# Three edits and a reordering in the front half of a fused attention and feed-forward kernel: V of one tile pair by seven products, separate PSUM tiles for the halves of a transpose, a narrower wait for one weight load, and VectorE's side work in another order

## The chip, the cores and the metric

The kernel runs on one core of a Trainium2 chip. The metric is the device time of one execution in microseconds (us); lower is better. TensorE (PE) multiplies matrices, VectorE (DVE) and ScalarE (ACT) work on rows of 128 partitions, GpSimd (POOL) and SyncE (SP) help, and DMAs are issued from SP's and ACT's queues. Matmuls write to PSUM, a small memory that VectorE and ScalarE must empty.

## The reference, cut to what matters

```python
def _A_ref(x, wqkv, wo):                      # linear attention, 32 heads of 32
    q, k, v = split(x @ wqkv)
    phi = lambda t: jnp.where(t > 0, t + 1, jnp.exp(t)) + 1e-6
    pq, pk = phi(q), phi(k)
    kv = einsum("bhsd,bhse->bhde", pk, v);  z = sum over s of pk
    o = (pq @ kv) / (pq . z + 1e-6)
    return o @ wo
def _B_ref(x, w_gate, w_up, w_down):
    return (silu(x @ w_gate) * (x @ w_up)) @ w_down
xn = layernorm(x)
out = x + _A_ref(xn, ...) * silu(_B_ref(xn, ...))
```

x is 2048 rows of 1024 in bf16; the feed-forward part is 3584 wide.

## The kernel before

There are three stages. The first normalises x, transposes it to xnT (the 1024 features on the partitions, two SBUF tiles of 1024 rows each), and computes K, V, the sums kv and z, and most of Q. The second computes the attention output o, writes it to DRAM, reads it back transposed (oT) and multiplies it by wo. The third is the feed-forward part, the longest; the change does not touch it.

The 2048 rows are 16 tiles of 128, in 4 blocks of 512. In the first stage a step on tile i is one of these:

- `emit_stats`, `emit_rstd`, `emit_N`: mean, variance and normalising, on VectorE.
- `emit_T(i)`: tiles 0 to 7 are transposed on TensorE, eight 128x128 transposes into the PSUM tile `tr_ps`; VectorE copies the first four of them to xnT (L423), ScalarE the other four (L424). Blocks 2 and 3 (tiles 8 to 15) go another way: `emit_xT_block` stores the normalised block to DRAM and a DMA transposes it back (L427, L428), both on SP's queue.
- `emit_B(i, c)`: one quarter of K and V for a tile, eight matmuls of 512 columns (L444) into a PSUM tile `kv_ps`. For K (c of 0, 1) ScalarE takes exp and relu (L186, L187) and VectorE makes phi of them (L190, L191); for V (c of 2, 3) ScalarE casts to `v_sb` (L462).
- `emit_C(i)`: eight matmuls of 129 columns (L473) that add phi(K)-transposed times V, and z, to the PSUM tiles `kvz`.

Tiles 0 to 8 and tile 12 are done so. For Q, and for the tile pairs (10,14) and (11,15) of K and V and (9,13) of K, the kernel saves an eighth of the matmuls: a 2x2 block product by seven products of half the depth instead of eight. `QGroup(p, m)` and `KVGroup(which, t)` are such groups; which = 0 is K, 1 is V, written K(t), V(t) and Q(p, m) here; Q(0, 2) is part 2 of the first half of the rows. Each product is four matmuls of 512 columns (L131), 28 for a group instead of 32. `part_a` makes M3 into X and M4 into Y, `part_b` M1 into Z and adds M5 to X and M2 to Y, `part_c` adds N7 to X and N6 to Y. Between them ScalarE copies X to `qu`, VectorE adds Y and Z to it (L236 and L241 for Q, L544 and L549 for K and V), ScalarE takes the two results that are done after M5 and M2, and VectorE subtracts for the other two after N7 and N6 (L251 for Q, L561 for K, L564 for V). A product that adds to X or Y has to wait until the readers before it are done.

The operands of these products are sums that VectorE makes ahead of time: five sums of x for each half of the rows (`xsum_ops`, L138), four of each of four wq parts (`wsum_ops`, L152 to L155), five of wk and five of wv (`kv_sum_ops`, L499 to L503). Places for them are found in SBUF that is no longer read; three of wv's lie in quarters of xnT. V of tiles 9 and 13 is computed by `VPlain`, which calls `emit_B` four times.

The order of the first two stages is written out by hand (`tc.manual_schedule`), and every engine keeps it. VectorE's side work (statistics and norms of blocks 2 and 3, then the sums) stands in a queue `later`; `put(weight, ops)` adds to it, and `fill(n)` gives credit and takes operations off while credit is left:

```python
        def fill(n):
            credit[0] += n
            while later and credit[0] > 0:
                weight, op = later.popleft()
                credit[0] -= weight
                op()
```

In the loop over `rest` (tiles 4 to 8 and 12), `fill` is called four times a tile with the numbers of `nf`; in the list `seq` each group has two numbers, `fa` after `part_a` and `fb` after `part_b`. In `seq` a group's `part_a` comes before the `part_c` of the group ahead of it, and `emit_C` of a pair follows when both its K and its V are ready (`have`).

PSUM in these two stages: pool `psA` has three buffers, `psB` five, each of one 2 KiB bank; kv_ps, tr_ps, the X, Y and Z of the groups and s_ps take turns in psB.

In the second stage the pools of the first are closed and new ones opened over the same SBUF: `wop` (for `wo_sb`), `p2oT` (for oT), `p2work`, `p2small`. By default a tile of a new pool waits for all that used the closed pools' space; with `reuse_waits="tile"` it waits for the users of its own place alone. `wo_sb` lies where `wk_sb` lay. SP's queue carries the two loads of `wo_sb` (L868) and then the transposing reads of oT (L831), whose data ACT's queue stores (L830). `emit_ND` makes o of a tile (`nd_ps`, `o_sb`), `emit_S` the product with wo (`s_ps`, L844).

Of the kernel before, what the change touches and what calls it, by code (L numbers as in the profile page):

```python
# [13 lines left out]
FP16 = mybir.dt.float16  # L14
# [7 lines left out]
def kernel(  # L22
# [12 lines left out]
    P = 128  # L35
# [175 lines left out]
    class QGroup:  # L211
# [17 lines left out]
        def part_a(self):  # L229
            self.X = psB.tile([P, CW], FP32, name="qX", tag="B")  # L230
            self.mm(self.X, "M3", True)
            self.u = qtmp.tile([P, CW], FP32, name="qu", tag="qu")
            nc.scalar.copy(out=self.u[:], in_=self.X[:])
            self.Y = psB.tile([P, CW], FP32, name="qY", tag="B")
            self.mm(self.Y, "M4", True)
            nc.vector.tensor_tensor(out=self.u[:], in0=self.u[:], in1=self.Y[:], op=ALU.add)  # L236
# [10 lines left out]
        def part_c(self):  # L247
            for acc, which, i in ((self.X, "N7", 0), (self.Y, "N6", 1)):
                self.mm(acc, which, False)
                e, r = self.er(i, i)  # L250
                nc.vector.tensor_tensor(out=r, in0=self.u[:], in1=acc[:], op=ALU.subtract)  # L251
                emit_exp_relu(e, r, r)
# [11 lines left out]
    with ExitStack() as p1:  # L264
# [136 lines left out]
        def emit_T(i):  # L401

            h = DC // 2
            dst = xn_tok_ap(i)
            xn = xn_slot(i)

            def tr(t_ps, dcs):
                for k, dc in enumerate(dcs):
                    nc.tensor.transpose(t_ps[:, k, :], xn[:, dc * P:(dc + 1) * P], ident[:])

            if i == 0:
                tr_a = psB.tile([P, h, P], FP16, name="tr_ps", tag="B")[:]
                tr_b = psB.tile([P, h, P], FP16, name="tr_ps", tag="B")[:]
                emit_norm(i, xn[:, 0:h * P], cols=slice(0, h * P))
                tr(tr_a, range(0, h))
                emit_norm(i, xn[:, h * P:D], cols=slice(h * P, D))
                tr(tr_b, range(h, DC))
                nc.scalar.copy(out=dst[:, 0:h, :], in_=tr_a)
                nc.scalar.copy(out=dst[:, h:DC, :], in_=tr_b)
            else:  # L420
                tr_ps = psB.tile([P, DC, P], FP16, name="tr_ps", tag="B")
                tr(tr_ps, range(DC))
                nc.vector.tensor_copy(out=dst[:, 0:h, :], in_=tr_ps[:, 0:h, :])  # L423
                nc.scalar.copy(out=dst[:, h:DC, :], in_=tr_ps[:, h:DC, :])  # L424

        def emit_xT_block(b):
            nc.sync.dma_start(out=blk_rows_pt(xn_dram, b), in_=xn_blk_slot(b))  # L427
# [37 lines left out]
        def emit_B(i, c):  # L465
            emit_B_mm(i, c)
            emit_B_out(i, c)
# [119 lines left out]
        def put(weight, ops):  # L587
            later.extend((weight, op) for op in ops)
# [19 lines left out]
        def put_sums():  # L608

            alloc_pqT()  # L610
            k_ops = kv_sum_ops(0, (pq_place(NPASS - 1, NM_Q - 2), pq_place(NPASS - 1, NM_Q - 1), x_quarter(0, 0, 1)))
            v_ops = kv_sum_ops(1, (x_quarter(0, 1, 0), x_quarter(1, 0, 1), x_quarter(1, 1, 0)))
            put(2, xsum_ops(0))
            put_ws(0)
            put_ws(1)
            put(2, xsum_ops(NPASS - 1))
            put(2, k_ops)
            put_ws(2)
            put(2, v_ops[:1])
            put_ws(3)  # L620
            put(2, v_ops[1:])

        put_stats(NB - 2)
        put(1, [lambda: emit_rstd((NB - 2) * TPB)])
# [6 lines left out]
        with tc.manual_schedule(engines=FRONT_ORDER | {ET.SP}):  # L631

            warm_up(14)
            emit_stats(0, parts=(0,))
            emit_stats(0, parts=(1,))
            emit_aggr(0)
            emit_rstd_act(0)
            emit_T(0)
            emit_stats(1)
            warm_up(2)  # L640
            emit_B_mm(0, 0)
            emit_rstd_act(1)
            nc.scalar.preload_act_table(ACT.Exp)
            emit_N(1)
            emit_T(1)
            ln(2)
            emit_B_mm(1, 0)
            emit_B_out(0, 0)
            emit_B_mm(0, 1)
            emit_B_out(1, 0)  # L650
            emit_B_mm(1, 1)
            ln(3)
            emit_N(2)
            emit_B_out(0, 1)
            emit_B_mm(0, 2)
            emit_T(2)
            emit_B_out(1, 1)
            emit_B_mm(1, 2)
            emit_B_out(0, 2)
            emit_N(3)  # L660
            emit_B_mm(2, 0)
            emit_B_out(1, 2)
            emit_B_mm(2, 1)
            emit_stats(TPB)
            emit_T(3)
            emit_stats(TPB + 1)
            emit_rstd(TPB)
            emit_B_out(2, 0)
            emit_B_mm(2, 2)
            emit_B_out(2, 1)  # L670
            emit_stats(TPB + 2)
            emit_B_mm(0, 3)
            emit_B_out(2, 2)
            emit_B_mm(1, 3)
            emit_B_out(0, 3)
            emit_stats(TPB + 3)
            emit_rstd(TPB + 2)
            emit_C(0)
            emit_B_mm(2, 3)
            emit_B_out(1, 3)  # L680
            emit_N(TPB)
            emit_N(TPB + 1)
            emit_C(1)
            emit_B_mm(3, 0)
            emit_B_out(2, 3)
            emit_C(2)
            emit_B_out(3, 0)
            emit_B_mm(3, 1)
            fill(4)
            emit_T(TPB)  # L690
            emit_B_out(3, 1)
            emit_N(TPB + 2)
            emit_N(TPB + 3)
            emit_B_mm(3, 2)
            emit_T(TPB + 1)
            emit_B_out(3, 2)
            fill(2)
            emit_B(3, 3)
            fill(2)

            rest = list(range(TPB, 2 * TPB)) + [b * TPB for b in range(2, NB)]
            fills = {rest[-1]: (2, 3, 2, 2)}
            before = TPB - 1
            for i in rest:
                nf = fills.get(i, (3, 2, 2, 2))
                grp = QGroup(0, 0) if i == rest[-1] else None
                emit_B(i, 0)
                fill(nf[0])
                emit_C(before)
                before = i  # L710
                if grp:
                    grp.part_a()
                emit_B(i, 1)
                fill(nf[1])
                if grp:
                    grp.part_b()
                if i == TPB:
                    emit_T(TPB + 2)
                emit_B(i, 2)
                fill(nf[2])  # L720
                if i == TPB:
                    emit_T(TPB + 3)
                if grp:
                    grp.part_c()
                emit_B(i, 3)
                if grp:
                    grp.post()
                fill(nf[3])

            K, V = (lambda t: KVGroup(0, t)), (lambda t: KVGroup(1, t))  # L730
            class VPlain:


                def part_a(self):
                    emit_B(tiles1[0], NCC)

                def part_b(self):
                    for i, c in ((tiles1[0], NCC + 1), (tiles1[1], NCC), (tiles1[1], NCC + 1)):
                        emit_B(i, c)

                def part_c(self):
                    have(tiles1)

                def post(self):
                    pass

            tiles1 = [(NB - 2 + j) * TPB + 1 for j in range(2)]
            Q = QGroup
            seq = [(lambda: Q(0, 1), 1, 1), (VPlain, 4, 6), (lambda: K(1), 1, 1), (lambda: Q(0, 2), 1, 1),
                   (lambda: V(2), 3, 3), (lambda: K(2), 1, 1), (lambda: Q(0, 3), 1, 0), (lambda: K(3), 0, 0),  # L750
                   (lambda: Q(NPASS - 1, 0), 0, 0), (lambda: V(3), 0, 0), (lambda: Q(NPASS - 1, 1), 0, 0)]
            prev = None
            for make, fa, fb in seq:
                grp = make()
                grp.part_a()
                fill(fa)
                if prev:
                    prev.part_c()
                    prev.post()
                else:  # L760
                    emit_C(before)
                if make is not seq[-1][0]:
                    grp.part_b()
                    fill(fb)
                while ready_C:
                    emit_C(ready_C.popleft(), last=(not ready_C and make is seq[-1][0]))
                prev = grp
            qa = prev
            assert not later
# [1 line left out]
        gate(wq_loads, marks[("B", 3)], sync=True)  # L771

    with ExitStack() as p2:
        wop = p2.enter_context(tc.tile_pool(name="wop", bufs=1))
        otp = p2.enter_context(tc.tile_pool(name="p2oT", bufs=1))
        work = p2.enter_context(tc.tile_pool(name="p2work", bufs=2))
        small = p2.enter_context(tc.tile_pool(name="p2small", bufs=2))
# [499 lines left out]
```

## Time and profile before

| | us |
|---|---|
| median of three runs | 756.86 (754.5 to 758.6) |
| the profiled execution | 754.58 |
| its span, first to last instruction | 752.8 |
| TensorE busy in the span | 744.0 |
| VectorE, ScalarE busy | 508.3, 276.1 |
| tile 4's C (the pause at kvz) | starts 49.48 |
| first product of Q, last C | 80.07, 158.15 |
| first product with wo | 171.79 |
| feed-forward part begins | 239.97 |

The granted clock of TensorE is 1.000 throughout. Times in the profile are counted from the first instruction. A matmul's record reaches beyond the start of the next, since they are pipelined (0.379 us each for 512 columns); what a stretch costs is seen from starts. A line "idle before <- X" or "waited for" names what ended the wait.

### The profile page before, as it was taken

The numbers are of one execution on the slowest core, as the hardware profiler recorded it, in microseconds if no ns is written. First come the engines' busy times: TensorE is split into PE (matmuls) and PEld (weight loads), VectorE is DVE, ScalarE is ACT, GpSimd is POOL, SyncE is SP. The second block draws the span as 40 slices with busy tenths as digits, with TensorE's granted clock in tenths as the row PEclk, the third lists the DMA queues.
The fourth block names the chain that finished last, engine by engine and source line by source line (L and its number), as shares of the span: only waits on it lengthen the run. The fifth ranks groups of instructions, "written<-read, shape, count | busy, mean of one in ns | idle before, by whom it ended". The sixth has DMA issues, their size and how long they took to land.

```text
span 752.8 us, 9958 instructions
## 1 busy us (share of the span) xinstructions
PE 744.0 (99%) x3744; PEld 350.2 (47%) x3744; DVE 508.3 (68%) x939; ACT 276.1 (37%) x483; POOL 51.1 (7%) x101
## 2 busy tenths in 40 slices
PE   9999999999999999999999999999999999999997
PEld 4544444454554444444444444444444444444454
DVE  6788887687754667886777767876755844445453
ACT  4444555754324434333343434343343111111111
POOL 3310000000000000000000000000000222122220
PEclk9999999999999999999999999999999999999999
DMA  9617000045589633764345733544869845554200
GB/s 313 221 39 211 1 1 0 1 137 144 173 226 293 175 104 106 203 182 124 107 147 163 220 100 105 175 148 129 286 227 347 304 181 182 181 182 167 99 29 29
DMA packets 127664, 115.99 MB, mean 154 GB/s; under 512 B 29440, under 2 KB 108416, under 8 KB 126336
## 3 DMA queue, kind: packets, MB, share of 16 engines
q1 hardware_dynamic: 122720, 106.58, 45.5%
q10 hardware_dynamic: 4896, 8.78, 3.3%
q8 instruction: 29, 0.48, 0.3%
q14 instruction: 19, 0.16, 0.1%
HBM read 70.52 MB, written 38.54 MB: 145 GB/s over the span
## 4 chain that ended last, share of the span: by engine, by line
PE 94%; DVE 3%; DMA 1%; ACT 1%; issue 0%; DVEq 0%; ACTq 0%
PE X L131 29%; PE Y L131 29%; PE Z L131 10%; PE kv_ps L444 9%; PE s_ps L844 7%; PE qY L131 2%; PE qX L131 2%; PE kX L131 2%; PE kY L131 1%; PE nd_ps L807 1%; PE kvz L473 1%; DVE stats L335 1%; PE w_ps L482 1%; DMA o_dram<-o_sb 1%; PE kZ L131 1%; PE qZ L131 1%
## 5 line engine op out<-in xcount | busy, mean ns | idle before, releaser
L131 PEld LDWEIGHTS <-ws_all 128*128 128x128 bf16 x1420 | 137.6, 98 | 161.8 <-issue 0.2
L940 DVE TENSOR_TENSOR q<-n,Y 128x512 f32<-128x512 f32 x63 | 43.4, 688 | 107.4 <-PE Y L131 103.9
L131 PEld LDWEIGHTS <-xs 128*128 128x128 bf16 (+1 forms) x716 | 67.6, 98 | 74.4
L1210 POOL TENSOR_TENSOR o_out<-y,xres 128x512 bf16<-128x512 f32 x29 | 35.2, 1215 | 665.9 <-DVE y L1209 665.9
L131 PE MATMUL Y<-xs,ws_all 128*128 128x512 f16 (+3 forms) x308 | 70.3, 360 | 0.0
L131 PE MATMUL X<-xnT,ws_all 128*128 128x512 f16 (+1 forms) x280 | 70.2, 379 | 0.0
L131 PE MATMUL X<-xs,ws_all 128*128 128x512 f16 x224 | 57.5, 379 | 0.0
L131 PE MATMUL Z<-xs,ws_all 128*128 128x512 f16 x224 | 57.5, 379 | 0.0
L131 PE MATMUL Y<-xnT,ws_all 128*128 128x512 f16 x224 | 57.5, 379 | 0.0
L1064 ACT ACTIVATE g<-cg 128x512 bf16<-128x512 f32 x56 | 35.3, 631 | 53.6 <-DVE cg L955 53.6
L946 DVE TENSOR_TENSOR u<-Z,q 128x512 f32<-128x512 f32 x63 | 43.2, 686 | 16.0 <-PE Z L131 15.9
L1064 ACT ACTIVATE g<-X 128x512 bf16<-128x512 f32 x28 | 16.7, 597 | 99.7 <-PE X L131 99.7
L444 PEld LDWEIGHTS <-xnT 128*128 128x128 f16 x352 | 33.7, 98 | 39.0 <-DVE xnT L423 0.7
L936 ACT COPY n<-X 128x512 f32<-128x512 f32 x63 | 36.9, 586 | 28.7 <-PE X L131 28.7
L444 PE MATMUL kv_ps<-wv_sb,xnT 128*128 128x512 bf16 x192 | 44.0, 379 | 0.0
L1089 DVE TENSOR_TENSOR ho<-g,up 128x1024 bf16<-128x1024 bf16 x56 | 38.2, 685 | 0.5
L444 PE MATMUL kv_ps<-wk_sb,xnT 128*128 128x512 bf16 x160 | 37.3, 379 | 0.5 <-DVE xnT L423 0.5
L1209 DVE TENSOR_TENSOR y<-y,s_in 128x512 f32<-128x512 f32 x31 | 22.2, 717 | 20.6 <-ACT y L1203 15.8
L131 PEld LDWEIGHTS <-wg_sb 128*128 128x128 bf16 x224 | 21.9, 98 | 26.4
L131 PEld LDWEIGHTS <-wu_sb 128*128 128x128 bf16 x224 | 21.9, 98 | 26.4
L848 ACT CAST s_sb<-s_ps 128x512 bf16<-128x512 f32 x32 | 18.5, 586 | 39.4 <-PE s_ps L844 33.0
L844 PE MATMUL s_ps<-wo_sb,oT 128*128 128x512 bf16 x128 | 29.4, 379 | 1.6 <-DMA oT<-o_dram 1.6
(179 smaller groups left out, 1109.0 us busy)
## 6 DMA issues: line engine op xcount, KB each, us to landing
h_dram<-ho SPq DMA_DIRECT2D x56, 256.0 KB, 2.5
wg_sb<-in_B_w_gate_dram SPq DMA_DIRECT2D x14, 512.0 KB, 4.0
wu_sb<-in_B_w_up_dram SPq DMA_DIRECT2D x14, 512.0 KB, 4.6
wdr<-in_B_w_down_dram SPq DMA_DIRECT2D x14, 512.0 KB, 4.2
ws_all<-h_dram SPq DMA_DIRECT2D x4, 1792.0 KB, 8.9
wds_dram<-wdsA SPq DMA_DIRECT2D x14, 384.0 KB, 2.8
hp_a<-h_dram SPq DMA_DIRECT2D x3, 1792.0 KB, 8.3
o_dram<-o_sb ACTq DMA_DIRECT2D x16, 256.0 KB, 3.0
```

What stands on the lines that cost most here:

```text
L131: marks["mm"] = nc.tensor.matmul(acc[:, 0:c1 - c0], lhsT=lhs(k), rhs=rhs(k)[:, c0:c1], start=(first and k == 0), stop=(k == n - 1), skip_g ...
L335: nc.vector.bn_stats(out=part_stats[i][:, c, :], in_=xr[:, c, :])
L444: mm = nc.tensor.matmul(kv_ps[:], lhsT=xn_tok_ap(i)[:, dc, :], rhs=wkv_ap(c)[:, dc, :], start=(dc == 0), stop=(dc == DC - 1))
L844: mm = nc.tensor.matmul(s_ps[:], lhsT=oT[:, c, ttok], rhs=wo_sb[:, c, cc * CW:(cc + 1) * CW], start=(c == 0), stop=(c == G - 1))
L848: nc.scalar.copy(out=s_sb[:, cc * CW:(cc + 1) * CW], in_=s_ps[:])
L936: nc.scalar.copy(out=n[:], in_=self.X[:])
L940: nc.vector.tensor_tensor(out=self.q[:], in0=n[:], in1=self.Y[:], op=ALU.add)
L946: nc.vector.tensor_tensor(out=self.u[:], in0=Z[:], in1=self.q[:], op=ALU.add)
L1064: nc.scalar.activation(out=self.g[:, i, j * TB:(j + 1) * TB], in_=src, func=ACT.Silu)
L1089: nc.vector.tensor_tensor(out=self.ho[:, i], in0=self.g[:, i], in1=self.up[:, i], op=ALU.mult)
L1209: nc.vector.tensor_tensor(out=t[:], in0=t[:], in1=self.s_in[:, i, cs], op=ALU.mult)
L1210: (nc.vector if last and (i, j) != (0, 0) else nc.gpsimd).tensor_tensor(out=self.o_out[:, i, cs], in0=t[:], in1=self.xres[:, i, cs], op=AL ...
```

## The change

- `emit_T` puts the two halves of a transpose in two PSUM tiles, each a buffer of psB, for all tiles but tile 0, where it was so already.
- `VPlain` is gone; V of tiles 9 and 13 is V(1), after Q(0, 2) in `seq`, and K(2), V(2), Q(0, 3) follow in a slightly different order. The order of `put_sums` has all five sums of wv ahead of the last wq part.
- `fills`, the default of `nf` and the numbers in `seq` give more credit in tiles 5 to 12 and less in `seq`.
- `wop` is opened with `reuse_waits="tile"`.

Line numbers of the changed kernel are higher by 2 behind `emit_T`, and lower by 16 in the second stage. On TensorE the order then has 3740 matmuls instead of 3744.

```diff
--- before.py
+++ after.py
@@ -418,10 +418,12 @@
                 nc.scalar.copy(out=dst[:, 0:h, :], in_=tr_a)
                 nc.scalar.copy(out=dst[:, h:DC, :], in_=tr_b)
             else:
-                tr_ps = psB.tile([P, DC, P], FP16, name="tr_ps", tag="B")
-                tr(tr_ps, range(DC))
-                nc.vector.tensor_copy(out=dst[:, 0:h, :], in_=tr_ps[:, 0:h, :])
-                nc.scalar.copy(out=dst[:, h:DC, :], in_=tr_ps[:, h:DC, :])
+                tr_a = psB.tile([P, h, P], FP16, name="tr_ps", tag="B")
+                tr_b = psB.tile([P, h, P], FP16, name="tr_ps", tag="B")
+                tr(tr_a, range(0, h))
+                tr(tr_b, range(h, DC))
+                nc.vector.tensor_copy(out=dst[:, 0:h, :], in_=tr_a[:])
+                nc.scalar.copy(out=dst[:, h:DC, :], in_=tr_b[:])
 
         def emit_xT_block(b):
             nc.sync.dma_start(out=blk_rows_pt(xn_dram, b), in_=xn_blk_slot(b))
@@ -616,9 +618,8 @@
             put(2, xsum_ops(NPASS - 1))
             put(2, k_ops)
             put_ws(2)
-            put(2, v_ops[:1])
+            put(2, v_ops)
             put_ws(3)
-            put(2, v_ops[1:])
 
         put_stats(NB - 2)
         put(1, [lambda: emit_rstd((NB - 2) * TPB)])
@@ -699,10 +700,10 @@
             fill(2)
 
             rest = list(range(TPB, 2 * TPB)) + [b * TPB for b in range(2, NB)]
-            fills = {rest[-1]: (2, 3, 2, 2)}
+            fills = {TPB: (3, 2, 2, 3), 2 * TPB: (5, 3, 2, 2), rest[-1]: (3, 4, 2, 2)}
             before = TPB - 1
             for i in rest:
-                nf = fills.get(i, (3, 2, 2, 2))
+                nf = fills.get(i, (3, 3, 2, 2))
                 grp = QGroup(0, 0) if i == rest[-1] else None
                 emit_B(i, 0)
                 fill(nf[0])
@@ -728,26 +729,9 @@
                 fill(nf[3])
 
             K, V = (lambda t: KVGroup(0, t)), (lambda t: KVGroup(1, t))
-            class VPlain:
-
-
-                def part_a(self):
-                    emit_B(tiles1[0], NCC)
-
-                def part_b(self):
-                    for i, c in ((tiles1[0], NCC + 1), (tiles1[1], NCC), (tiles1[1], NCC + 1)):
-                        emit_B(i, c)
-
-                def part_c(self):
-                    have(tiles1)
-
-                def post(self):
-                    pass
-
-            tiles1 = [(NB - 2 + j) * TPB + 1 for j in range(2)]
             Q = QGroup
-            seq = [(lambda: Q(0, 1), 1, 1), (VPlain, 4, 6), (lambda: K(1), 1, 1), (lambda: Q(0, 2), 1, 1),
-                   (lambda: V(2), 3, 3), (lambda: K(2), 1, 1), (lambda: Q(0, 3), 1, 0), (lambda: K(3), 0, 0),
+            seq = [(lambda: Q(0, 1), 1, 0), (lambda: K(1), 1, 0), (lambda: Q(0, 2), 1, 1), (lambda: V(1), 2, 2),
+                   (lambda: K(2), 0, 0), (lambda: V(2), 2, 1), (lambda: Q(0, 3), 0, 0), (lambda: K(3), 0, 0),
                    (lambda: Q(NPASS - 1, 0), 0, 0), (lambda: V(3), 0, 0), (lambda: Q(NPASS - 1, 1), 0, 0)]
             prev = None
             for make, fa, fb in seq:
@@ -771,7 +755,7 @@
         gate(wq_loads, marks[("B", 3)], sync=True)
 
     with ExitStack() as p2:
-        wop = p2.enter_context(tc.tile_pool(name="wop", bufs=1))
+        wop = p2.enter_context(tc.tile_pool(name="wop", bufs=1, reuse_waits="tile"))
         otp = p2.enter_context(tc.tile_pool(name="p2oT", bufs=1))
         work = p2.enter_context(tc.tile_pool(name="p2work", bufs=2))
         small = p2.enter_context(tc.tile_pool(name="p2small", bufs=2))
```

## The prediction

> **What bounds the kernel now.** I read the page first, for the busy shares and the chain that ended last:
>
> ```profile
> PE 744.0 (99%) x3744; PEld 350.2 (47%) x3744; DVE 508.3 (68%) x939; ACT 276.1 (37%) x483; POOL 51.1 (7%) x101
> PE 94%; DVE 3%; DMA 1%; ACT 1%; issue 0%; DVEq 0%; ACTq 0%
> ```
>
> TensorE is idle for 8.8 us of the span, 1.2 of them before the first matmul and about 4.9 behind the last. Only fewer matmuls, or a shorter pause between two of them, can shorten the run. The view of who waited for whom names the pauses, with SyncE's long wait from the DMA queue's own:
>
> ```profile
> ACT xnT L424 <- DVE xnT L423: 14.6, 7, 3.3
> PE s_ps L844 <- DMA oT<-o_dram: 1.6, 1, 1.6
> PE kv_ps L444 <- DVE xnT L423: 0.5, 1, 0.5
> PE kvz L473 <- ACT v_sb L462: 0.5, 1, 0.5
> SPq L868 <- PE kvz L473: 86.4, 1, 86.4
> ```
>
> TensorE's timeline shows each at its place (start, us, what, idle before):
>
> ```profile
> 9.25 0.61 PE L409 MATMUL tr_ps<-ident,ws_all 128*128 128x128 f16 x8
> 10.38 5.35 PE L444 MATMUL kv_ps<-wk_sb,xnT 128*128 128x512 bf16 x24 [0.52 <-DVE xnT L423]
> ...
> 49.48 0.39 PE L473 MATMUL kvz<-v_sb,pk_sb 128*128 128x129 bf16 x4
> 50.37 0.39 PE L473 MATMUL kvz<-v_sb,pk_sb 128*128 128x129 bf16 x4 [0.50 <-ACT v_sb L462]
> 50.60 1.89 PE L444 MATMUL kv_ps<-wk_sb,xnT 128*128 128x512 bf16 x8
> ...
> 115.06 1.36 PE L473 MATMUL kvz<-v_sb,pk_sb 128*128 128x129 bf16 x16
> 116.26 1.02 PE L131 MATMUL kX<-wv_sb,xs 128*128 128x512 bf16 x4
> ...
> 169.21 1.02 PE L131 MATMUL qY<-xs,ws_all 128*128 128x512 f16 x4
> 171.79 1.90 PE L844 MATMUL s_ps<-wo_sb,oT 128*128 128x512 bf16 x8 [1.55 <-DMA oT<-o_dram]
> ```
>
> Four 512-column matmuls start 0.864 us apart (kX to kY), 0.216 each; a kvz matmul or a transpose takes 0.058 (eight in 0.46). The loss is counted in starts, not in the idle column. The kvz at 49.48 take 1.12 instead of 0.46: 0.66 lost. The sixteen at 115.06 take 1.20 instead of 0.93: 0.27, and the same again at 134.39 (1.20). From 169.21 to 171.79 stand 2.58 instead of 0.86: 1.72. The chain of waits tells why the last is so long:
>
> ```profile
> 163.45 4.98 DMA o_dram<-o_sb
> 168.44 3.30 DMA oT<-o_dram
> 171.79 1.90 PE s_ps L844 x8
> ```
>
> **Part by part.** *Seven products for tiles 9 and 13.* Four plain blocks of 8 matmuls become 28: four fewer, 4 x 0.216 = 0.86 us off the path, for certain. VectorE gets four operations of 0.69 more (2.4 us at their spacing of 0.61), ScalarE one evacuation less; beside 6.0 us of matmuls they hide, if the queues are not already late (below). All five sums of wv existed for tiles 10, 11, 14, 15; they only come earlier.
>
> *Two PSUM tiles per transpose.* ScalarE's half no longer waits for VectorE's. At 47.52 ScalarE had stood 2.83 us for it with tile 4's v_sb behind, which makes the pause at 50.37: 0.66 back. For tile 1 VectorE's half starts four transposes sooner (4 x 0.058): 0.23 back. A transpose now takes two of psB's five buffers. The tightest reuse is the block that starts at 46.03: it needs the buffer of the transpose at 43.41, whose copy follows ScalarE's pair at 43.61 and 44.10 and ends near 45.2. It costs nothing, with 0.6 us to spare; without that cover, one copy of 0.59.
>
> *wo by tile.* The load lies where wk_sb lay. It waited for all of the earlier pools, that is for the last kvz (issue at 158.70), and then ran beside the first store of o_sb, which took 4.98; the view of DMA issues gives such stores 2.1 at best and a median of 2.4 up to 180. Waiting for its own place alone, it leaves after K(3)'s last product with wk_sb, which starts at 144.22: 13 us sooner, into a stretch with a DMA share of 0.01. SyncE has nothing behind it until the transpose at 168.44, which inherits the pool's waits; those end with that kvz too, ten us before its data. The store then lands at 163.45 + 2.4, oT 3.3 later: 169.2, where TensorE is ready at 170.07. All 1.72 go; with a store as slow as before, none. What is late next is oT of the second tile: transpose issued near 170.5, landed by 173.8, wanted at 178.04 - 1.72. [...]
>
> *The accumulations of two tiles.* C of tiles 9 and 13 stood right behind K(1)'s phi and lost 0.27; now V(1) stands between, and at 134.39 likewise V(2) before Q(0,3). Between V(1)'s last product and C stand K(2)'s 12 matmuls, 2.6 us, while its two subtractions need 1.5, so 0.54 are back; if they came late, nothing.
>
> Gains: 0.86 + 0.66 + 0.23 + 1.72 + 0.54 = 4.0.
>
> *Side work sooner.* The order of the instructions shows what moves in front of what; VectorE and ScalarE wait in their places. Two spots have no spare:
>
> ```profile
> 92.59 0.57 ACT L462 CAST v_sb<-kv_ps 128x512 bf16<-128x512 f32 x1
> 93.02 0.62 PE L473 MATMUL kvz<-v_sb,pk_sb 128*128 128x129 bf16 x8
> 123.09 0.57 ACT L535 CAST v_sb<-kX 128x512 bf16<-128x512 f32 x1
> 124.03 1.03 PE L131 MATMUL kX<-wv_sb,xs 128*128 128x512 bf16 x4
> ```
>
> (a) C of tile 12: its fifth matmul needs the cast that ends at 93.16, and starts at 93.25. Between tile 12's phi and the subtraction L251 that ScalarE follows, VectorE had three sums of 1.14 (their spacing, five in 5.76); now two sums and four parts of a w sum (0.34 + 0.60 + 0.34 + 0.34): 3.90 against 3.42. So 0.48 later, 0.09 of it spare: 0.4 lost.
> (b) V(1)'s N7 must wait until ScalarE has read kX. Chain from the end of K(1)'s M4: to VectorE's qu 0.27, qu 0.61, a sum of wv that now stands there 1.14, L251 0.69; ScalarE's four steps from SBUF 2.38, four from PSUM 1.92, copy 0.62; VectorE from L236 to L241 4.45 (111.02 to 115.65 less a wait of 0.18), then 0.60, a sum 1.14, qu 0.61, a sum 1.14, L251 0.71; ScalarE's four 2.38, cast 0.57; handshakes 0.11. Together 19.3. TensorE has 84 matmuls in between, 18.1: 1.2 lost. Before, the plain V blocks stood ahead of this stretch, and sixteen kvz (1.20) inside it.
>
> Bounds of both together: 0, as in the rows above, where both arrive in time, and 2.7, if one more sum (1.14) stands ahead of ScalarE. I take 1.6, the sum of the chains, since each link is a row. [...]
>
> Sum: -4.0 + 1.6 = -2.4. The profiled execution, 754.58 (span 752.8 and 1.8 around it), becomes 752.2. It lies 2.3 under the median of the three runs, 756.86; on that median the forecast is **754.5**.
>
> **Rivals.** *No new waits:* -4.0, 752.9. For it: VectorE idles 1.79 at 75.26 and 1.18 at 53.16, room to get ahead. Against: it is 82% busy from 80 to 120.
> *The store stays slow:* -2.4 + 1.72 = -0.7, 756.2. For it: nothing but that the first store is also the first of its kind; against: the DMA share.
> *VectorE becomes the bound from tile 8 to V(2):* the sums of the second x half (L138) now stand four in a row ahead of tile 8's phi. The second needs the transposed block 3, which landed at 68.18 + 6.1 = 74.3. If it does not land sooner, phi ends at 74.3 + 3 x 1.14 + 1.2 = 78.9, against C of tile 8 at 79.61 - 0.89 = 78.7, and all that is later comes one for one onto TensorE. If then each of wv's five sums (5.7) and the four parts of a w sum (1.6) stand ahead of what ScalarE waits for, 7.3 are lost: +3.3, 760.2. It decides from 4.0 us of new waits. Against: block 2's norms now stand ahead of a phi, so its store and all behind it leave up to 2.3 us sooner.
> *The change does not do what it says:* the wait of wo could still hold it, or tiles 9 and 13 save nothing; the order shows four matmuls fewer and the wait on wk_sb's last reader, so 756 at most.
>
> **How the numbers follow.** Forecast 0.42, no new waits 0.32, slow store 0.10, VectorE 0.12, not as said 0.04. A measurement of this kernel can tell about 0.5% from no change, 3.8 us; the three runs alone lie 4.1 apart. The forecast is 1.4 short of that bound, so some 0.3 of it would be read as faster, and 0.6 of the second case: 0.13 + 0.19, rounded to 0.33. Slower takes a little over half of VectorE's case: 0.07. The rest, 0.60, is the same. The range goes from the second case less two us of scatter, 750.8, to the slow store with 1.4 above, 757.6; it leaves out VectorE's case and the ends of the scatter.
>
> **What would show it.** Right: 3740 matmuls; wo's issue near 144; no pause before the first s_ps; no wait of xnT L426 for VectorE; kvz at tile 4 in 0.46; new pauses at tile 12's C and at V(1)'s N7. Wrong: pauses of over 4 us in all between 75 and 120, a first store near 5 us, or TensorE waiting for a psB buffer between 35 and 50.

## The result and the profile after

The changed kernel takes 752.41 us, the median of six runs (752.04 to 752.71). The kernel before, run beside it, takes 757.73 (six runs, 754.5 to 758.6). The ratio is 0.9938, 95% interval 0.9921 to 0.9956: 0.6% shorter. The forecast was 754.5 with a range of 750.8 to 757.6; the profiled execution, forecast at 752.2, took 752.22 (span 750.4 against 752.8).

So there are two results. The step from the one profiled execution to the other is 2.4 us, as worked out. The step between the medians is 5.3, and 2.9 of it were not foreseen. The busy times on the page of the changed kernel:

```profile
PE 741.2 (99%) x3700; PEld 350.0 (47%) x3740; DVE 510.0 (68%) x943; ACT 274.9 (37%) x482; POOL 51.6 (7%) x101
```

The weight loads (PEld) show the 3740 matmuls; 40 matmul records are missing from this trace. The view of waits, TensorE's and ScalarE's (what waited, for what, us in total, times, longest):

```profile
PE kX L131 <- ACT v_sb L537: 0.6, 1, 0.6
PE kv_ps L446 <- DVE xnT L425: 0.3, 1, 0.3
PE kvz L475 <- ACT v_sb L464: 0.3, 1, 0.3
...
ACT xnT L426 <- PE tr_ps L409: 8.5, 5, 3.1
```

The wait of s_ps for oT is gone, and so is every wait of ScalarE's half of a transpose for VectorE's. What is left at kvz is another tile's wait than before, and the one at kX is new. TensorE's timeline gives the places, and SyncE's the load and the first transpose:

```profile
49.30 0.63 PE L475 MATMUL kvz<-v_sb,pk_sb 128*128 128x129 bf16 x8
...
92.18 0.39 PE L475 MATMUL kvz<-v_sb,pk_sb 128*128 128x129 bf16 x4
92.84 0.39 PE L475 MATMUL kvz<-v_sb,pk_sb 128*128 128x129 bf16 x4 [0.27 <-ACT v_sb L464]
...
116.76 1.02 PE L131 MATMUL kX<-wv_sb,xs 128*128 128x512 bf16 x4 [0.57 <-ACT v_sb L537]
...
168.62 1.02 PE L131 MATMUL qY<-xs,ws_all 128*128 128x512 f16 x4
169.48 1.89 PE L828 MATMUL s_ps<-wo_sb,oT 128*128 128x512 bf16 x7
```

```profile
144.69 1.01 SPq L852 DMA_DIRECT2D wo_sb<-in_A_wo_dram  x2
165.44 1.24 SPq L815 DMA_TRANSPOSE oT<-o_dram  x1
```

Tile 4's C runs through, and C of tiles 9 and 13 takes 0.93 (it starts at 121.07, the next product at 122.00). Tile 12's C loses 0.43 (from 92.18 to qZ at 93.07 are 0.89 instead of 0.46). The product N7 of V(1) starts 1.60 behind kY, which starts at 115.16, instead of 0.86: 0.74 lost, the largest of five delays in that stretch. And s_ps follows qY after 0.86, where it was 2.58: wo's load leaves at 144.69, the first store at 163.14, and the transpose 2.30 behind that, where it was 4.98. In windows of 2 us from 160 to 166 the DMA share, 0.99, 1.07 and 1.05 in the kernel before, is 0.00, 0.02 and 0.34; from 146 to 152 it is 0.88, 1.03 and 1.09.

### The profile page after: what moved, and what is told of

Its sections match the earlier page's. It is cut to its first block, busy times and chain, and to the rows that moved or that the text cites. A ratio compares the mean times of both kernels' runs of the same rounds, so it can differ in the third digit from the quotient of the medians.

```text
span 750.4 us, 9920 instructions
## 1 busy us (share of the span) xinstructions
PE 741.2 (99%) x3700; PEld 350.0 (47%) x3740; DVE 510.0 (68%) x943; ACT 274.9 (37%) x482; POOL 51.6 (7%) x101
## 4 chain that ended last, share of the span: by engine, by line
PE 95%; DVE 2%; ACT 1%; issue 1%; DVEq 0%
PE X L131 29%; PE Y L131 29%; PE Z L131 10%; PE kv_ps L446 8%; PE s_ps L828 7%; PE qY L131 2%; PE qX L131 2%; PE kY L131 2%; PE kX L131 2%; PE nd_ps L791 1%; PE kvz L475 1%; PE w_ps L484 1%; PE qZ L131 1%; PE kZ L131 1%; PE tr_ps L409 0%
## 5 line engine op out<-in xcount | busy, mean ns | idle before, releaser
L131 PEld LDWEIGHTS <-xs 128*128 128x128 bf16 (+1 forms) x736 | 69.6, 98 | 77.8 <-issue 1.4
L446 PEld LDWEIGHTS <-xnT 128*128 128x128 f16 x320 | 30.5, 98 | 35.0 <-ACT xnT L418 0.5
L446 PE MATMUL kv_ps<-wv_sb,xnT 128*128 128x512 bf16 x155 | 36.4, 379 | 0.2
L1187 ACT ACTIVATE y<-X 128x512 f32<-128x512 f32 x8 | 4.8, 597 | 69.7 <-PE X L131 61.2
```

What stands on the lines that cost most here:

```text
L131: marks["mm"] = nc.tensor.matmul(acc[:, 0:c1 - c0], lhsT=lhs(k), rhs=rhs(k)[:, c0:c1], start=(first and k == 0), stop=(k == n - 1), skip_g ...
L446: mm = nc.tensor.matmul(kv_ps[:], lhsT=xn_tok_ap(i)[:, dc, :], rhs=wkv_ap(c)[:, dc, :], start=(dc == 0), stop=(dc == DC - 1))
```

## The experiments

What had to be explained is the 2.9 us that the profiles don't show, and the scatter: the runs of before lay 4.1 apart, those of the changed kernel 0.7. **Theory A**: the pause ahead of the first s_ps is of another length in every execution, and the profiled one was a short one. **Theory B**: the terms of the profile hold in every run, and the rest comes from another part of the change.

The first four kernels shared a chip. There the kernel before took 755.07 (32 runs, 753.91 to 758.38).

**wo by tile alone**, on the kernel before:

```diff
-        wop = p2.enter_context(tc.tile_pool(name="wop", bufs=1))
+        wop = p2.enter_context(tc.tile_pool(name="wop", bufs=1, reuse_waits="tile"))
```

> The kernel before with one edit, wo's pool waiting by tile. The profiled executions of before and after differ by 2.4 us, the timed medians by 5.3 (757.7 against 752.4), and the runs of before lie 4.1 apart, those of after 0.7. Theory A (the store): what varies in before is the first o_sb store, which shares the DMA engines with wo's load; its profiled execution, 754.58, was a lucky one. Then this edit alone removes the scatter and more than 1.72 us: 5.3 less the 0.7 that the rest of the change is worth in the profile gives 4.6, about 753.1, with runs within 1 us. Theory B (the terms of the profile hold in every run, and what else the medians differ by belongs to another part of the change or to how the runs were taken): 1.7 off, about 756.0, and the scatter of some 4 us stays. Both: the load leaves near 144, the store lands in about 2.1 to 2.4, no pause before the first s_ps.

753.12 (752.68 to 753.58), ratio 0.9966 [0.9952, 0.9981]. The scatter is gone with this edit alone, as theory A says. The gain is 1.95 on this chip, close to theory B's 1.7; the 4.6 of theory A were counted from the first set, where before stood higher. In the profiled execution the four stores up to 176 land a median of 2.7 behind their issue, later than the 2.1 to 2.4 expected, and s_ps still follows qY after 0.86.

**All but wo**: the changed kernel with that one line taken back.

> The changed kernel with wo's pool waiting for all the earlier pools again, all else as changed. Theory A: 4.6 slower than after, about 757.0, and the runs 3 to 4 us apart as those of before; the pause before the first s_ps is back and is as long as the store is late. Theory B: 1.7 slower than after, about 754.1, and runs within 1 us of one another.

756.21 (753.92 to 756.54), ratio 0.9998 [0.9983, 1.0013]: without wo's edit nothing is left of the gain. In the profiled executions the last qY starts 0.51 sooner than in the kernel before (168.70 against 169.21), but the first s_ps 0.21 later (172.00 against 171.79): what the first stage gains goes into the pause. Theory A again, but the runs showed more than it had said. They do not spread; they stand in two groups, four at 753.9 to 754.1 and seven at 756.2 to 756.5, with one at 755.6. The mean granted clock of the upper group is 0.996 to 0.997, that of the others 0.998 to 1.000. This mean tells a drop in one direction only: the profiled execution with the transposes alone (below) has 0.998, and its eight s_ps behind the pause take 1.90, as without a drop. It also counts time without work: in the trace of the changed kernel the clock is 0.91 from 748.0 to the end of the span at 750.4, where no matmul runs. By an estimate from the windows below (1.66 us of clock missing in a span of 754.6), one drop like that is worth 0.002. So, by the same estimate, 0.996 and 0.997 show a drop, and 0.998 neither shows nor excludes one. The profiled execution, 756.37, is of the upper group. Its chain of waits, and the view of windows (start and end, length, busy time of PE, PEld, DVE, ACT, POOL with the number of instructions, then TensorE's granted clock, DMA share, GB/s):

```profile
163.21 5.07 DMA o_dram<-o_sb
...
168.29 3.65 DMA oT<-o_dram
...
172.00 3.52 PE s_ps L828 x8
```

```profile
172.00:174.00 2.00, 2.00 (x5) 0.72 (x6) 0.00 (x0) 0.90 (x2) 0.00 (x0) 0.50 0.56 177
174.00:176.00 2.00, 2.00 (x13) 1.02 (x12) 0.26 (x2) 0.44 (x1) 0.00 (x0) 0.67 0.12 29
```

TensorE was idle for 2.27 us here, and behind that its clock was 0.50 from 172 to 174, 0.67 in the next window and 1.00 from 176 on: the first eight s_ps took 3.52 instead of 1.89. The pause is paid once as waiting, 2.44 from start to start, and once more as 1.63 of slow matmuls; together 4.07, where this execution and that of the changed kernel lie 4.15 apart (756.37 and 752.22).

**The transposes alone**: the kernel before with the first hunk of the change.

> The kernel before with the transposed tiles in two PSUM tiles alone. Its two terms are 0.66 at tile 4's accumulation (kvz start to start 0.46 instead of 1.12) and 0.23 at tile 1's first product. Theory A: 0.9 off, about 756.8, scatter as in before. Theory B with the transposes as what steadies the runs: 0.9 and up to 2.9 more, about 753.9, with runs within 1 us.

753.96 (753.08 to 756.38), ratio 0.9984 [0.997, 0.9999]. That is 1.1 under the kernel before on this chip (by the interval 0.1 to 2.3), with its scatter: the size of the term, 0.9, agrees, and theory B's steadying is not there. One of its runs took 756.38 at a mean clock of 1.000: part of the scatter has no drop in it. The absolute figures expected belonged to the first set, where before stood higher.

**The kernel before again.**

> The kernel before, unchanged, for its scatter and for a second profiled execution. Theory A: again 754 to 759; the profiled execution of whatever length has its first store at 4.98 plus what its span has over 752.8, and the pause before the first s_ps at 1.55 plus the same. Theory B: where its span is longer, the additional time stands at other places (x's first loads, or PE's clock), and the first store takes 5 as before.

754.85 (753.97 to 758.09). The profiled execution, 753.97, has the shorter pause that theory A asks for, 0.45 under the 1.55 of the first profile, with a span 0.6 shorter and a store of 4.56 instead of 4.98:

```profile
171.20 1.90 PE L844 MATMUL s_ps<-wo_sb,oT 128*128 128x512 bf16 x8 [1.10 <-DMA oT<-o_dram]
```

This gave two new theories. **C**: a pause costs twice once it is long enough, as the 2.27 was and the 1.10 and 1.55 were not, through the clock. **D**: the clock is only a sign of a long pause, whose length explains all. Two experiments put work in the pause, and one made pauses of known length. Filler in the kernel before (on a chip where that took 754.91, 17 runs, 753.9 to 757.61):

```diff
+            f_ps = psB.tile([P, CW], FP32, name="f_ps", tag="B")
+            for _ in range(8):
+                nc.tensor.matmul(f_ps[:], lhsT=warm[:, 0:P], rhs=warm[:], start=True, stop=True)
             rows = deque((grp, i) for grp in (qa, qb, qc) for i in range(2))
```

> The kernel before with eight more 512-column matmuls that nobody reads, between the last qY product and the first s_ps, where TensorE waits for oT: 1.73 us of work in the pause. In the trace of the changed kernel without wo's edit the idle of 2.27 there was followed by a granted clock of 0.50 to 0.67 for some three microseconds, and eight s_ps matmuls took 3.52 instead of 1.89; after idles of 1.10, 1.16 and 1.55 in other traces the clock stayed at 1.00. Theory C (the pause costs twice: itself, and a clock that halves once it is longer than about two): with the filler the idle that is left is at most 2.2 even in the longest runs, the clock stays at 1.00, the runs of before that lay at 756.3 to 758.4 come down by 1.6, and the short ones go up by up to 0.6 (1.73 of filler against an idle of 1.1 to 1.5): all of them from 754.2 to 756.8, median about 755. Theory D (the scatter is the store's length alone, the clock only a sign of it): short runs up by up to 0.6, the long ones stay at 756.3 to 758.4.

755.66 (754.33 to 756.83), ratio 1.0006 [0.9993, 1.0018], no run with a clock under 0.998. The range is the one of theory C, but only 3 of the 17 runs of before lay above 756.83, too few to decide. The median is 0.7 above that of before: where the pause is short, the filler only delays. And runs of 756.83, 756.44 and 756.23 had a clock of 0.999 or 1.000, with no room for a drop by that estimate, so some 2.5 us of scatter come without the clock. Wo by tile alone took the scatter away, so it should be the pause's length, which was not measured run by run.

**Pauses of known length**, in the feed-forward part of the changed kernel, ahead of M3 of every second group:

```diff
+        nc.tensor.matmul(acc[:, 0:P], lhsT=warm[:, 0:P], rhs=pz[:, 0:P], start=True, stop=True)
+        ...  # GpSimd adds to pz over 128 to 1536 columns
+        nc.tensor.matmul(acc[:, 0:P], lhsT=warm[:, 0:P], rhs=pz[:, 0:P], start=True, stop=True)
```

> The changed kernel with 32 pauses of TensorE in the feed-forward, one ahead of every second group (some 12 us apart), each as long as GpSimd takes for additions over 128, 256, 384, 512, 640, 768, 1024 and 1536 columns, in turn, four times; a short matmul on either side holds the pause. From the row of o_out (512 columns in 1.21) they are some 0.5 to 4 us long, 55 to 60 us in all. Theory C: behind pauses of up to 1.55 the granted clock stays at 1.00 and the next four matmuls start 0.86 apart; behind the longest it drops to 0.50 and costs about 1.6 more each; in between lies the limit, between 1.55 and 2.27, sharp or not. With the 768, 1024 and 1536 columns over the limit, twelve drops of 1.6, 19 us on top of the pauses. Theory D: no drop follows a pause as such; the time is that of the pauses alone.

846.58, one run; 68.5 us of it are the idle time of the 32 pauses. TensorE's timeline behind two pauses of the same 2.10 (lines left out at the dots):

```profile
306.66 0.22 PE L925 MATMUL X<-pz,warm 128*128 128x128 bf16 x1 [2.10 <-POOL pz L923]
...
307.58 1.79 PE L131 MATMUL Y<-xs,wg_sb 128*128 128x512 f16 x4
...
311.85 1.03 PE L131 MATMUL Z<-xs,ws_all 128*128 128x512 f16 x4
...
424.63 0.22 PE L925 MATMUL X<-pz,warm 128*128 128x128 bf16 x1 [2.10 <-POOL pz L923]
...
425.54 1.03 PE L131 MATMUL Y<-xs,wg_sb 128*128 128x512 f16 x4
```

Behind the first, the twelve matmuls from 307.58 to 311.85 take 4.27 instead of 2.59: 1.68 lost, with a granted clock of 0.92, 0.50 and 0.72 in the windows of 2 us from 306 to 312 and of 1.00 in the next. Behind the second, nothing: its groups of four start 0.86 to 0.87 apart. Over all pauses, counted from the starts of the 25 matmuls behind each:

| idle of TensorE, us | pauses | with a drop | each costs |
|---|---|---|---|
| 0.69 to 1.35 | 16 | 0 | 0 |
| 1.86 to 1.98 | 4 | 0 | 0 |
| 2.10 | 3 | 1 | 1.68 |
| 2.64 to 2.71 | 3 | 2 | 1.68, 1.69 |
| 3.81 | 3 | 3 | 1.40, 1.68, 2.80 |
| 5.48 to 7.19 | 3 | 3 | 1.70, 1.81, 2.17 |

Nine drops cost 16.6, where twelve and 19 were expected; the last three pauses came out longer than asked for, which was not followed up. Why equal pauses end differently was not shown. What the execution shows is that no pause of up to 1.98 was followed by a drop, three of the six of 2.10 to 2.71 were, and all six from 3.81 on were. The 2.27 of the kernel without wo's edit, with its drop, lies in the range where both were seen.

**Filler where the two groups were plain**: the changed kernel without wo's edit, with the same eight matmuls (a chip where before took 754.96, 18 runs, six of them from 756.38 to 758.34 with a clock of 0.996 or 0.997).

> The changed kernel without wo's edit, whose runs fell into two groups, four at 753.9 to 754.1 and seven at 756.2 to 756.5 (and one at 755.6), now with eight 512-column matmuls that nobody reads in the pause ahead of the first s_ps. In the 32 measured pauses none of up to 1.98 us of idle was followed by a lower clock, three of six at 2.09 to 2.71 were, and all of 3.81 and more, at 1.4 to 2.8 us each, 1.68 in the middle. Theory C: the filler leaves at most 0.6 of the idle of 2.27, the clock stays at 1.00, and the upper group comes down by 1.6 to about 754.7; all runs from 753.9 to 755. More work gives less time. Theory D (the upper group is the store's length alone): two groups as before, some 2.3 apart, none of them faster.

754.30 (753.57 to 754.97), ratio 0.9982 [0.9971, 0.9994], the clock 0.998 or more in all twelve runs. The upper group is gone, and in eight of the runs the clock is 0.999 or more, with no room for a drop; 1.73 us of work that nobody reads made the median 1.9 shorter than the 756.21 without it (measured on another chip; against before, the ratio went from 0.9998 to 0.9982). The profiled execution, 754.97, shows how (timeline):

```profile
169.50 1.89 PE L867 MATMUL f_ps<-warm 128*128 128x512 bf16 x8
172.21 1.90 PE L828 MATMUL s_ps<-wo_sb,oT 128*128 128x512 bf16 x8 [0.81 <-DMA oT<-o_dram]
```

By its chain of waits the store took 5.41 and the transpose 3.58, together more than the 5.07 and 3.65 in the execution of 756.37. The wait was there, 2.71 with the filler in it, from start to start; the drop was not. Against 4.07 for both that is 1.36 less, and the run was 1.4 shorter. For the two groups theory C holds; the length of the pause, all that theory D has, makes the spread in which the clock has no part.

**The parts on TensorE's path.** On that same chip, the changed kernel without the seven products of V(1) and their side work:

> The changed kernel without the seven products for tiles 9 and 13 and without their side work, that is, the kernel before with the two PSUM tiles and wo by tile. By the terms of the prediction those products gain 0.86 + 0.54 and their waits cost 1.6, so that this part is worth +0.2: here 752.2 against 752.4 for the changed kernel. By the start of the last qY ahead of s_ps in two traces (168.18 with the transposes alone, 168.70 with the products too) it costs 0.5: 751.9. Rival (the two new waits hide in slack that ends elsewhere, and the four matmuls and the accumulations count in full): 753.8.

752.27 (751.68 to 753.23), ratio 0.9955 [0.9939, 0.9971]. And the changed kernel beside it:

> The changed kernel itself, on the same chip as the others of this set: 752.4, runs within 0.7 us of one another, clock 1.00 in each.

752.27 (751.86 to 752.59), ratio 0.9955 [0.9939, 0.9971]. The part that gave the change its first words is worth nothing that can be measured. Executions start unevenly (the first kv_ps between 7.25 and 8.15), so the traces are compared from there to the last qY ahead of s_ps: 161.70 before, 160.87 with the transposes alone, 160.77 with the transposes and wo, 161.04 in the changed kernel. The products and their waits cost 0.2 to 0.3, forecast 0.2.

**The two waits.** One sum of wv moved ahead, into an idle time of VectorE of 2.12 us:

```diff
-            seq = [(lambda: Q(0, 1), 1, 0), (lambda: K(1), 1, 0), ...
+            seq = [(lambda: Q(0, 1), 1, 1), (lambda: K(1), 0, 0), ...
```

> The changed kernel with one of wv's sums moved ahead: behind Q(0,1)'s part b instead of inside K(1), so that it falls into VectorE's idle of 2.12 us ahead of qu at 97.68. The theory of the prediction (the chain of VectorE and ScalarE from K(1)'s M4 to V(1)'s N7, 19.3 against 18.1 of matmuls, makes the wait): the chain loses a sum, 1.14, the five waits between 103 and 117 shrink from 1.22 to some 0.1, time 751.3. Rival (VectorE as a whole is the bound in this stretch, or what is gained is lost at a later wait): the wait moves to another product, kX or qX before 103 or C of tile 13 behind 117, and the time stays within 0.3 of 752.4.

751.18 (751.0 to 752.11), ratio 0.9945 [0.9929, 0.9961]. The five delays shrink from 1.22 to one of 0.28, ahead of V(1)'s N7 (the kY before it starts at 114.40); wait (a) stays:

```profile
115.54 1.02 PE L131 MATMUL kX<-wv_sb,xs 128*128 128x512 bf16 x4
```

Both waits:

```diff
-            fills = {..., rest[-1]: (3, 4, 2, 2)}
+            fills = {..., rest[-1]: (3, 3, 2, 2)}
-            seq = [(lambda: Q(0, 1), 1, 0), (lambda: K(1), 1, 0), ...
+            seq = [(lambda: Q(0, 1), 2, 1), (lambda: K(1), 0, 0), ...
```

> The changed kernel with both waits attended to: tile 12 takes one part less of a w sum between its phi and L251, and Q(0,1) takes two credits and one instead of one and none, so that a sum of wv falls into VectorE's idle. By the two chains of the prediction: wait (a), 0.4 at tile 12's C, and wait (b), 1.2 before V(1)'s N7, both go but for 0.1: 750.9, 1.5 under the changed kernel. Rival: the part of a w sum that tile 12 gives up stands ahead of another reader and waits there (0.3 to 0.4 back, 751.3), or all of it is given back (752.4).

750.99 (750.74 to 751.29), ratio 0.9941 [0.9925, 0.9956]. Tile 12's C runs in one piece, and nothing took the waits' place. These two ran on the filler's chip, where the changed kernel was not run; in the traces the way from the first kv_ps to the last qY goes from 161.04 to 160.15 and 159.64:

```profile
92.31 0.62 PE L475 MATMUL kvz<-v_sb,pk_sb 128*128 128x129 bf16 x8
92.78 1.02 PE L131 MATMUL qZ<-xs,ws_all 128*128 128x512 f16 x4
```

And with Q(0, 2) at (1, 3) and V(1) at (0, 2) besides:

> The kernel with both waits attended to, and with the sums of wv that stood between V(1)'s part a and L251 moved ahead of V(1)'s part a (Q(0,2) takes one credit and three, V(1) none and two), so that the last wait, 0.28 ahead of V(1)'s N7, goes too. Theory of the chains: 750.7, 1.7 under the changed kernel on the same chip, and no pause of TensorE between 70 and 130. Rival (VectorE is full in this stretch and the sums now delay Q(0,2)'s subtraction): 0.4 to 1.1 back, 751.1 to 751.8.

750.64 (750.34 to 751.27), ratio 0.9935 [0.9919, 0.9951], on the chip where the changed kernel took 752.27: 1.6 faster than it, and the best version here. From the first kv_ps to the last qY it takes 159.56 where the changed kernel took 161.04. The last wait went from 0.28 to 0.20, not to nothing.

## Why the prediction was right and where it was wrong

**Right: the terms, on the profiled execution.** 3740 matmuls. 0.66 at tile 4's C: its kvz take 0.46. The transposes: 0.83 from first kv_ps to last qY, forecast 0.89. Two times 0.27 at C(9,13) and C(10,14): both take 0.93. wo: issued at 144.69, the transpose issued 2.30 behind the first store, 1.72 back. Wait (a) 0.43 for a forecast of 0.4, wait (b) 1.22 (from 97.41, the end of K(1)'s M4, to 116.76 are 19.35, against 18.13 of matmuls) for 1.2 from the chain of 19.3. The experiments confirm the two chains from the other side: taking a link out of each gave the time back.

**Wrong: the step from that execution to the median.** "It lies 2.3 under the median of the three runs; on that median the forecast is 754.5" carried the scatter of before over to the changed kernel as a fixed amount. The scatter was not a property of the runs; it was made in the place that the change removes. The same kernel with wo alone runs within 0.9, and the changed kernel without it within 2.6.

**Mis-sized with it: wo's term.** 1.72 is its worth in an execution without a drop and with a pause of 1.55. Where the pause is longer it is worth more, and where the clock drops behind it 1.63 on top in the one such execution profiled. Measured by itself, between medians, the edit is worth 1.95 on one chip (755.07 to 753.12). In the first set, where five of six runs of before lay above 756.8, the medians leave 5.3 less 0.7 for the rest of the change: 4.6, worked out and not measured alone. The prediction read the clock as 1.000 in one trace and gave no price to what happens when a pause grows. The store itself, 2.4 in the forecast, took 2.30 up to the transpose in this execution; in that with wo's edit alone the four stores up to 176 took a median of 2.7 up to their landing.

**The rivals.** No new waits, 752.9, came closest to the measured median for a reason that did not hold: both waits came, and the time was lower for another cause. The slow store did not happen. VectorE did not become the bound: the sum of x waited 1.2 us for block 3, no more. That "the same" was held the likeliest comes from the same step: 0.9938 is past the bound of half a percent. On the last chip, where fewer runs of before were long, the same two kernels give 0.9955.

**Open.** Why the first store beside wo's load takes 4.26 to 5.41 us and not one time, and why five of six runs of before were long in the first set (756.86 and more) and only 16 of 67 had a clock under 0.998 in the later ones (3 of 12 in the kernel before again), was not tried. No long run of the kernel before was profiled: for its runs of 757 to 758.6 the drop is inferred from the mean clock and from the trace of 756.37, and how long their pauses were is not known.

## What to carry to other kernels

If a kernel's runs scatter and one profile is at hand, look for the wait in it that depends on a race between transfers, and ask what it costs when it is longer; a change that removes it removes the scatter too, so the gain is counted against the median of the runs and not against the profile. Pauses of TensorE are not all alike: of the 32 measured here none of up to 1.98 us was followed by a lower clock, and all six from 3.81 on were, at 1.40 to 2.80 each. Filler makes them shorter if nothing better is at hand, but it costs where most pauses are short (0.7 on the median of the kernel before). Side work on VectorE is placed by the chain of what stands behind it: moving small pieces gave back 1.4 us of the 1.65 that the new products had taken in waits.

## What the runs showed of the hardware

Behind a pause of 2.27 us TensorE's granted clock was 0.50 from 172 to 174 and 0.67 from 174 to 176, in the kernel without wo's edit; eight matmuls took 3.52 instead of 1.89. Of 32 pauses in one execution none up to 1.98 led to a drop, all six from 3.81 on did, and of three of 2.10 one did. These drops cost 1.40 to 2.80 us. What decides between equal pauses was not shown. The first 256 KB store beside wo's 2 MB took 4.26, 4.56, 4.86, 4.98, 5.07 and 5.41 us in six profiled executions, from its issue to that of the transpose, and 2.30 in that of the changed kernel, in which that load had gone ahead.
